# Wider value products, repeated score columns and filler matmuls in a decode attention kernel

## The chip, the cores and the metric

The kernel runs on 1 core of one Trainium2 chip. The metric is the time of one execution on the device in microseconds (us), the median over runs. The profile's span, from the first instruction to the last, is about 2 us shorter than that time.

In the views of the profile PE is TensorE's matmuls, PEld its weight loads, DVE VectorE, ACT ScalarE and POOL GpSimd. "Issue" is time in which the profile shows nothing that the engine waits for. The granted clock is the share of TensorE's full speed that the chip lets it run at; in the clock records of before it is 1.0 or 0.5 and nothing else, in pieces of 3.41 us. "Cold" in the recorded texts is a clock of 0.5. A chunk is 16 of the 64 value products of a unit, one for each quarter of V.

## The reference

Two attention blocks, A and B, decode one token for 4 sequences. Each has 32 query heads and 8 key/value heads of width 128, and a cache of 8192 positions. A uses all positions, B only the last 2048. The outputs are concatenated.

```python
q = (x @ wq)                                   # B, 32 heads, 1, 128
scores = einsum("bhqd,bhkd->bhqk", q, k) * Dh ** -0.5
p = softmax(scores)
o = einsum("bhqk,bhkd->bhqd", p, v)
out = o @ wo                                   # for A and for B, then concatenated
```

There is little arithmetic: the caches that must be read are 168 MB of the 184.6 MB that the kernel reads.

## The kernel before

The work is cut into 40 units: 8 of B and then 32 of A. A unit of A is one sequence and one key/value head: 2 MB of K and 2 MB of V. Four K and four V buffers are filled by one DMA queue, in the order of the units. A unit goes through these steps:

- 32 transposes, which take pairs of bf16 numbers as fp32, bring K into the form that the score product needs; VectorE and ScalarE copy the results to `KT_sb` in turns;
- 64 score products, each with 128 columns of K as weights and 8 query columns streaming;
- softmax over the positions (VectorE, ScalarE, GpSimd);
- 64 value products, each with a 128x128 tile of V as weights and **4** probability columns streaming.

Every product loads new weights (1590 matmuls and 1589 weight loads from 200 to 300 us). TensorE takes the steps of a unit in one fixed order, with the value products of the unit before woven in:

```python
# pe_S: scores
ins = pe.matmul(out=stb[:, t * CPT:(t + 2) * CPT], lhsT=ktv[:, pi, :, e],
                rhs=rhs, start=(e == 0), stop=(e == 1))        # rhs: RQc[:, u % Bn, e, :], 8 columns
# pe_PV: values; CPT is 4 for A
for i in range(TQ):
    t = c * TQ + i
    s, j = t // J, t % J
    ins = pe.matmul(out=otb[:, s * CPT:(s + 1) * CPT], lhsT=V_sb[:, vs, t, :],
                    rhs=pt_cols(u, t * CPT, CPT), start=(j == 0), stop=(j == J - 1))
# (cut) order of TensorE in a unit:
TOKENS = [("T", 0), ("T", 1), ("OT",), ("T", 2), ("T", 3), ("S", 0), ("S", 1), ("X",),
          ("T", 4), ("T", 5), ("S", 2), ("S", 3), ("PV", 0), ("PV", 1), ("OL",),
          ("T", 6), ("T", 7), ("S", 4), ("S", 5), ("PV", 2), ("PV", 3), ("S", 6), ("S", 7), ("OPJ",)]
# (cut) after the last unit L = 39:
for c in range(NQ):
    pe_PV(L - 1, c)
add(dve_norm(L - 1))
for c in range(NQ):          # the V of the last unit comes in four quarters, one DMA each
    pe_PV(L, c)
add(dve_norm(L))
pe_OPJ(L // Bn)              # output projection of the last group: 8 matmuls of 256 columns
```

The body (units 10 to 37) is a hardware loop on TensorE; units 38 and 39 and the end are written out.

## Time and profile before

| | before |
|---|---|
| time, median of 3 runs | 450.13 us |
| span of the profile | 447.8 us |
| mean granted TensorE clock | 0.797 of full |
| DMA share from 50 to 400 us | 1.00 to 1.01 |
| last quarter of V lands (semaphore of its last of 16 parts) | 440.63 us |
| from there to the end | 7.14 us |

From the page of the kernel before: the granted clock and the DMA share in 40 slices (tenths), the summary of the chain that ended last, and two groups (busy us, mean ns of one; then the idle time before them and what ended it). L332 is the transpose, L397 the value product.

```profile
PEclk9996569989886899866596689867875986788596
DMA  8999999999999999999999999999999999999991
...
DMA 54%; PE 35%; issue 4%; ACT 3%; DVE 2%; POOL 0%; ACTq 0%; POOLq 0%
...
L332 PE MATMUL ps<-identf,K_sb 128*128 128x128 f32 x1280 | 217.1, 329 | 32.9 <-DMA K_sb<-in_A_k_cache_dram 17.5
...
L397 PE MATMUL ps<-PT,V_sb 128*128 128x4 bf16 (+1 forms) x2560 | 76.2, 165 | 3.6 <-DMA V_sb<-in_A_v_cache_dram 1.8
```

DMA is full (9 tenths or more) in every slice but the first and the last. The chain is 54% DMA. TensorE is busy too, but it sat idle for 17.5 us before transposes because K was not there: in the body it waits for the stream. The mean of a transpose is 329 ns, which counts time that overlaps with its neighbours (1280 times 329 ns are 421 us, and the group was busy for 217.1 us) and mixes two clocks.

The table of stretches of the kernel before (first column the stretch, then its length, the busy time of each engine with the number of instructions, the granted clock, the DMA share and GB/s):

```profile
core 0: us, PE busy (x) PEld busy (x) DVE busy (x) ACT busy (x) POOL busy (x), PEclk, DMA share, GB/s
200.00:300.00 100.00, 91.00 (x1590) 85.02 (x1589) 44.59 (x103) 43.45 (x50) 9.01 (x29) 0.76 1.01 428
300.00:400.00 100.00, 91.90 (x1660) 84.16 (x1656) 44.40 (x102) 44.23 (x51) 9.69 (x31) 0.77 1.01 428
413.00:427.00 14.00, 13.65 (x174) 11.51 (x175) 5.43 (x14) 3.98 (x6) 0.94 (x3) 0.52 1.00 426
427.00:440.00 13.00, 11.87 (x255) 11.23 (x253) 7.70 (x17) 8.41 (x10) 1.71 (x5) 1.00 0.85 349
440.00:448.00 8.00, 5.17 (x126) 4.10 (x126) 2.08 (x7) 0.42 (x1) 0.46 (x2) 0.50 0.01 3
```

Through the body the stream runs at 428 GB/s. Look at 413 to 427: TensorE is busy 13.65 of 14 us and its clock is 0.52. It has work, and it does it at half speed, just before the end. From 440 on nothing is loaded any more and the kernel still needs almost 8 us.

The timeline of the kernel before, at the end, transposes of the last unit (L332), value products (L397), normalisation (L592), output projection (L474) and final addition (L812):

```profile
start us, us, engine line op out<-in xcount [idle before <-releaser]
...
431.81 2.08 PE L332 MATMUL ps<-identf,K_sb 128*128 128x128 f32 x16
...
438.96 0.39 PE L397 MATMUL ps<-PT,V_sb 128*128 128x4 bf16 x10
...
440.17 3.31 PE L397 MATMUL ps<-PT,V_sb 128*128 128x4 bf16 x118 [0.82 <-issue]
...
443.52 0.17 DVE L592 TENSOR_TENSOR OTg<-ps,RL 128x4 bf16<-128x4 f32 x1 [1.33 <-PE ps L397]
...
443.79 1.86 PE L474 MATMUL ps<-W,OTg 128*4 128x256 bf16 x8 [0.31 <-DVE OTg L592]
...
445.69 0.41 DVE L812 TENSOR_TENSOR xo_sb<-ps,oacc 4x256 bf16<-4x256 f32 x1 [0.44 <-PE ps L474]
```

The last K had landed at 425.79, and its transposes begin only at 431.81. The last V is there at 440.63. TensorE begins its last 118 value products at 440.17 and needs until 443.48 for them, at about 28 ns each. The 0.82 us of "issue" before them come on top. Then the projection takes 1.86 us at half clock.

### The profile page before, as it was taken

The page shows a single profiled execution, that of the slowest core. Times are in us where ns is not written, and L with a number is a line of the kernel's source. Part 1 is how long each engine was busy: PE and PEld are TensorE (multiplying, and loading weights), DVE is VectorE, ACT ScalarE, POOL GpSimd, SP SyncE. Part 2 cuts the span into 40 slices and gives each one's busy share as a digit, 9 for nine tenths or more (in the row PEclk, how much of TensorE's full clock was granted, in tenths as well). Part 3 has the DMA queues.
Part 4 walks back from the last instruction along what each step waited for, and adds up shares of the span by engine and source line. Part 5 has one row for each costly group of instructions (what it writes and reads, how often), then busy time and mean ns, then how long its engine had stood idle before and what let it go on. Part 6 is the DMA issues. An engine that isn't in the chain of part 4 may idle for free.

```text
span 447.8 us, 14767 instructions
## 1 busy us (share of the span) xinstructions
PE 373.4 (83%) x6783; PEld 339.4 (76%) x6783; DVE 195.9 (44%) x451; ACT 179.2 (40%) x202; POOL 40.1 (9%) x126
## 2 busy tenths in 40 slices
PE   0685199899676999988998998899889998988997
PEld 0685199768561898878898887879878987878896
DVE  0354055656440455434363444344443544344363
ACT  1163045435330464434264434334442543435261
POOL 1100000001100011000010001000110100010010
PEclk9996569989886899866596689867875986788596
DMA  8999999999999999999999999999999999999991
GB/s 337 411 415 438 413 421 415 420 421 423 423 422 421 425 422 425 424 429 427 427 427 430 430 424 426 430 428 427 429 426 427 426 430 429 426 424 430 430 403 65
DMA packets 17270, 185.01 MB, mean 413 GB/s; under 512 B 1860, under 2 KB 2392, under 8 KB 4824
## 3 DMA queue, kind: packets, MB, share of 16 engines
q1 hardware_dynamic: 15096, 178.27, 94.4%
q10 hardware_dynamic: 2080, 6.30, 3.5%
q8 instruction: 22, 0.36, 0.3%
q14 instruction: 8, 0.07, 0.0%
q0 software_dynamic: 64, 0.01, 0.0%
HBM read 184.56 MB, written 0.01 MB: 412 GB/s over the span
## 4 chain that ended last, share of the span: by engine, by line
DMA 54%; PE 35%; issue 4%; ACT 3%; DVE 2%; POOL 0%; ACTq 0%; POOLq 0%
DMA K_sb<-in_A_k_cache_dram 41%; PE ps L332 19%; DMA W<-in_A_wq_dram 7%; DMA W<-in_B_wo_dram 6%; PE ps L397 6%; PE ps L371 5%; PE ps L483 3%; ACT KT_sb L341 3%; PE ps L278 1%; DVE KT_sb L340 1%; DVE Dt L543 0%; DVE M L505 0%; ACT PT L554 0%; PE ps L474 0%; PE ps L438 0%
## 5 line engine op out<-in xcount | busy, mean ns | idle before, releaser
L341 ACT ACTIVATE KT_sb<-ps 128x1024 bf16<-128x1024 bf16 x160 | 163.0, 1023 | 244.9 <-PE ps L332 243.1
L332 PE MATMUL ps<-identf,K_sb 128*128 128x128 f32 x1280 | 217.1, 329 | 32.9 <-DMA K_sb<-in_A_k_cache_dram 17.5
L332 PEld LDWEIGHTS ps<-identf,K_sb 128*128 128x128 f32 x1280 | 179.0, 170 | 46.2 <-DMA K_sb<-in_A_k_cache_dram 18.6
L340 DVE COPY KT_sb<-ps 128x512 int32<-128x512 int32 x160 | 110.4, 690 | 138.9 <-PE ps L332 137.7
L397 PE MATMUL ps<-PT,V_sb 128*128 128x4 bf16 (+1 forms) x2560 | 76.2, 165 | 3.6 <-DMA V_sb<-in_A_v_cache_dram 1.8
L371 PEld LDWEIGHTS ps<-RQc,KT_sb 128*128 128x128 bf16 x2048 | 72.9, 100 | 4.5 <-ACT KT_sb L341 1.2
L371 PE MATMUL ps<-RQc,KT_sb 128*128 128x8 bf16 x2048 | 74.3, 167 | 0.9 <-ACT KT_sb L341 0.8
L397 PEld LDWEIGHTS ps<-PT,V_sb 128*128 128x128 bf16 x2560 | 70.8, 97 | 3.9 <-DMA V_sb<-in_A_v_cache_dram 2.0
L575 POOL PARTITION_ALL_REDUCE LB<-L x40 | 17.3, 432 | 155.2 <-DVE L L566 155.2
L514 POOL PARTITION_ALL_REDUCE MB<-M x32 | 11.9, 371 | 173.3 <-DVE M L505 173.3
L483 PE MATMUL ps<-W,OL 128*4 128x512 bf16 x60 | 22.5, 537 | 4.8 <-DMA W<-in_B_wo_dram 4.8
L592 DVE TENSOR_TENSOR OTg<-ps,RL 128x4 bf16<-128x4 f32 (+1 forms) x40 | 6.9, 173 | 40.2 <-PE ps L397 40.2
L505 DVE TENSOR_REDUCE M<-ps 128x4 f32<-128x256 f32 (+1 forms) x40 | 19.1, 477 | 10.8 <-PE ps L371 10.8
L566 DVE TENSOR_REDUCE L<-PT 128x4 f32<-128x256 bf16 (+1 forms) x40 | 21.9, 547 | 3.3 <-ACT PT L554 2.8
L371 PE MATMUL ps<-RQB,KT_sb 128*128 128x16 bf16 x512 | 18.6, 171 | 2.1 <-issue 1.2
L371 PEld LDWEIGHTS ps<-RQB,KT_sb 128*128 128x128 bf16 x512 | 17.9, 99 | 3.0 <-issue 1.5
L554 ACT ACTIVATE PT<-Dt 128x256 bf16<-128x256 f32 (+1 forms) x40 | 18.1, 452 | 4.0 <-DVE Dt L543 2.0
L483 PEld LDWEIGHTS ps<-W,OL 128*4 128x4 bf16 x60 | 5.6, 104 | 15.3 <-issue 8.7
L278 PE MATMUL ps<-xT,W 128*128 128x4 bf16 x256 | 7.4, 165 | 10.9 <-DMA W<-in_A_wq_dram 10.6
L278 PEld LDWEIGHTS ps<-xT,W 128*128 128x128 bf16 x256 | 7.0, 101 | 11.1 <-DMA W<-in_A_wq_dram 10.7
L543 DVE TENSOR_TENSOR Dt<-ps,MB 128x256 f32<-128x256 f32 x32 | 13.3, 415 | 0.5 <-POOL MB L514 0.5
L257 PE MATMUL ps<-ident,xo_sb 4*128 4x4 bf16 x8 | 0.6, 170 | 14.2 <-POOL identf L617 14.2
(49 smaller groups left out, 64.6 us busy)
## 6 DMA issues: line engine op xcount, KB each, us to landing
K_sb<-in_A_k_cache_dram SPq DMA_DIRECT2D x32, 2048.0 KB, 32.0
V_sb<-in_A_v_cache_dram SPq DMA_DIRECT2D x31, 2048.0 KB, 36.0
K_sb<-in_B_k_cache_dram SPq DMA_DIRECT2D x16, 1024.0 KB, 28.2
V_sb<-in_B_v_cache_dram SPq DMA_DIRECT2D x16, 1024.0 KB, 28.2
W<-in_B_wq_dram SPq DMA_DIRECT2D x1, 4096.0 KB, 12.9
W<-in_A_wq_dram SPq DMA_DIRECT2D x1, 4096.0 KB, 30.0
W<-in_A_wo_dram ACTq DMA_DIRECT2D x8, 512.0 KB, 10.5
W<-in_B_wo_dram SPq DMA_DIRECT2D x1, 2048.0 KB, 29.1
```

The source lines that it names most:

```text
L278: ins = pe.matmul(out=bk[:, hl * Bn:(hl + 1) * Bn], lhsT=W1wq[:, c, hq * DH:(hq + 1) * DH], rhs=xT[:, P, c, :], start=(c == 0), stop=(c == ...
L332: ins = pe.transpose(out=bkf[:, pi * 128:(pi + 1) * 128], in_=K_sbf[:, slot, t0:t0 + 2, :].rearrange("p t d -> p (t d)"), identity=identf[ ...
L340: return e.tensor_copy(out=KT_sb.bitcast(I32)[:, tj % NKT, :], in_=bkf.bitcast(I32)[:, :])
L341: return e.activation(out=KT_sb[:, tj % NKT, :], in_=bk[:, :], func=ACTF.Copy)
L371: ins = pe.matmul(out=stb[:, t * CPT:(t + 2) * CPT], lhsT=ktv[:, pi, :, e], rhs=rhs, start=(e == 0), stop=(e == 1))
L397: ins = pe.matmul(out=otb[:, s * CPT:(s + 1) * CPT], lhsT=V_sb[:, vs, t, :], rhs=pt_cols(u, t * CPT, CPT), start=(j == 0), stop=(j == J - 1))
L483: ins = pe.matmul(out=opb[0:Bn, 0:D], lhsT=OL[:, i // REP, i % REP, :], rhs=wo_view[:, wg + i // REP, i % REP, :], start=(P == 1 and first ...
L505: return dve.tensor_reduce(out=M1[:, 0:NC].rearrange("p (s h) -> p s h", h=CPT), in_=stb[:, 0:NT * CPT].rearrange("p (s j h) -> p s h j", ...
L543: return dve.tensor_tensor(out=Dt[:, 0:NT * CPT].rearrange("p (s j h) -> p s j h", s=S, h=CPT), in0=stb[:, 0:NT * CPT].rearrange("p (s j h ...
L554: return act.activation(out=PT[:, u % NPT, 0:NW], in_=Dt[:, 0:NW], func=ACTF.Exp, scale=scale)
L566: return dve.tensor_reduce(out=L1[:, 0:NC].rearrange("p (s h) -> p s h", h=CPT), in_=PT[:, u % NPT, 0:NT * CPT].rearrange("p (s j h) -> p ...
L575: return pool.partition_all_reduce(LB[:, 0:NC], L1[:, 0:NC], channels=128, reduce_op=ReduceOp.add)
```

## The change

The intent: keep TensorE's granted clock up by letting it stream more columns. The value product streams 64 columns instead of 4; only the first 4 of each 64 output columns mean anything. The A score product repeats its 8 query columns 4 times (32 columns); the surplus output is overwritten by the next product. Two matmuls of 512 columns whose result nobody reads ("fillers") stand after each of the first three chunks of the last unit.

```diff
+    NW = 64
+    NR = 4
-        PT = sb("PT", [128, NPT, NT * 2 * REP], BF16)
+        PT = sb("PT", [128, NPT, NT * 2 * REP + NW], BF16)
 ... (cut: filler(), pe_filler(n): n matmuls of 512 columns into a free bank)
-                            rhs = RQc[:, u % Bn, e, :]
+                            rhs = RQc[:, u % Bn, e:e + 1, :].broadcast_to([128, NR, 2 * CPT])
+                            dst = stb[:, t * CPT:(t + 2 * NR) * CPT].rearrange("p (a c) -> p a c", a=NR)
-                    ins = pe.matmul(out=otb[:, s * CPT:(s + 1) * CPT], lhsT=V_sb[:, vs, t, :],
-                                    rhs=pt_cols(u, t * CPT, CPT), start=(j == 0), stop=(j == J - 1))
+                    ins = pe.matmul(out=otb[:, s * NW:(s + 1) * NW], lhsT=V_sb[:, vs, t, :],
+                                    rhs=pt_cols(u, t * CPT, NW), start=(j == 0), stop=(j == J - 1))
 ... (cut: normalisation reads every 64th group; PT is set to 0 at the start)
         for c in range(NQ):
             pe_PV(L, c)
+            if c < NQ - 1:
+                pe_filler(2)
```

## The prediction

> **What bounds the kernel now.** The DMA stream. The table of stretches shows DMA share 1.00 to 1.01 and 414 to 428 GB/s from 50 to 400 us. The chain of waits is 54% DMA. A unit's K and V land every 10.1 us. TensorE waits for K in 13 units (17.5 us, view of waits). So TensorE time matters only at the end. The last quarter of V lands at 440.6 us; the span is 447.8. In those 7.2 us (timeline): TensorE is behind, still issuing the last 118 narrow value products at 440.17 to 443.48 (28 ns each); normalisation 0.17; output projection 1.86 at half clock; addition to 446.10; output DMA about 1.7.

> **What changes.**
> - Value product, 64 per unit: 4 columns to 64. Now 32 take 0.80 us. [...]
> - A score product, 64 per unit: 8 to 32 columns. 16 take 0.38 us now[...].
> - Fillers: 6 matmuls of 512 columns, two after each of the last unit's first three chunks[...]. V quarters land at 436.9, 438.1, 439.4 and 440.6[...].
> - One memset on GpSimd, 128x2304: about 2.3 us (512 columns took 0.52). It may delay the first transposes, but loads are queued about 28 us ahead: worth 0.

> **Critical path.** The stream is untouched: last landing stays at 440.6 +-0.5. [...] TensorE still waits for K and the clock will still drop sometimes, but for fewer pieces: mean clock from 0.80 to about 0.88. That is off the path. In the tail, TensorE should have done all but the last chunk when it lands: chunk to 441.15, normalisation to 441.4, projection at full clock about 1.0 to 442.45, addition to 442.9, output to 444.6. Gain about 3.2 us: 2.3 from the backlog, 0.85 from the projection.

> **Prediction: 447.0 us, 8 in 10 within 445.8 to 449.0.** Faster by over 2%: 0.01; within 2%: 0.96; slower by over 2%: 0.03.

> **What the profile would show.** Right: last V landing near 440.6; granted clock 1.00 from about 427 to the end; the chain ending with the V DMA, then 16 value products, projection about 1.0 us. Wrong: a clock of 0.5 at the projection; more than one chunk of value products after the last landing; fillers delaying chunks; slices with DMA below 9.

> **What would make it wrong.** If in cold stretches wide products[...] cost more than the activity buys back, TensorE falls behind before 427 us and the tail keeps its length: about 450. [...] the gain shrinks to the 1 to 2 us that the fillers give. [...]

The forecast's sum came to a gain of 3.2 us, from a span of 447.8 to one of 444.6: 2.3 of backlog and 0.85 of projection. None of them is a term of the 3.2 us by itself, but the 0.55 us that the forecast gives the last chunk seems to lean on the first. It stands, as does the 1.0 us for a projection that took 1.86 us at half clock, as the author's estimate (measured: 0.64 and 1.03).

What the two traces show, as medians from one start to the next within a piece of the clock: a product of 4 or 8 columns 25 ns at full clock and 27 at half, one of 32 columns 25 and 27, one of 64 columns 29 and 53, one of 512 columns 215 to 217 and 427. A transpose takes 109 and 213 ns, as does a product of 256 columns in the projection; so the count of a transpose as 256 columns fits its time. Whether the chip counts it so is not shown.

## The result, and the profile after

The ratio is the mean time of one kernel's runs over that of the other's of the same rounds, so not quite the ratio of the medians that stand beside it. Executions over 1.5% slower than the fastest of the same kernel are left out of the means.

| | before | after |
|---|---|---|
| time, median of 4 runs each (before: the three above and one more) | 450.04 us (448.51 to 450.60) | 447.92 us (447.24 to 448.72) |
| ratio | | 0.9961, 95% interval 0.9939 to 0.9982 |
| span of the profiled run | 447.8 us | 445.2 us |
| mean granted clock | 0.797 | 0.942 |
| last V lands | 440.63 us | 441.03 us |
| from there to the end | 7.14 us | 4.16 us |
| value products begun after that landing | 101 | 16 |
| output projection | 1.86 us | 1.03 us |

The same parts of the page after (L348 is now the transpose, L414 the value product):

```profile
PEclk9998579999976899989899899999899999999999
DMA  8999999999999999999999999999999999999993
...
DMA 57%; PE 32%; issue 4%; ACT 3%; DVE 3%; POOL 1%; ACTq 0%; POOLq 0%
...
L348 PE MATMUL ps<-identf,K_sb 128*128 128x128 f32 x1280 | 183.8, 292 | 36.0 <-DMA K_sb<-in_A_k_cache_dram 19.5
...
L414 PE MATMUL ps<-PT,V_sb 128*128 128x64 bf16 x2560 | 90.4, 195 | 17.5 <-DMA V_sb<-in_A_v_cache_dram 16.1
```

DMA is as full as before. The clock is mostly full. A transpose takes 292 ns on average instead of 329, which is 33 us less in the sum of transposes; a value product, 195 instead of 165. Almost none of these 33 us shows in the time, because the stream sets the pace in the body: instead, TensorE now also waits 16.1 us for V.

The same stretches after:

```profile
core 0: us, PE busy (x) PEld busy (x) DVE busy (x) ACT busy (x) POOL busy (x), PEclk, DMA share, GB/s
200.00:300.00 100.00, 82.47 (x1622) 75.81 (x1620) 45.04 (x105) 43.69 (x50) 9.50 (x31) 0.97 1.01 428
300.00:400.00 100.00, 80.80 (x1618) 74.92 (x1618) 43.30 (x99) 43.58 (x50) 9.01 (x29) 0.98 1.01 427
413.00:427.00 14.00, 12.76 (x226) 11.30 (x226) 7.48 (x20) 7.21 (x9) 1.51 (x5) 1.00 1.02 431
427.00:440.00 13.00, 12.29 (x295) 11.41 (x294) 6.74 (x16) 5.79 (x7) 1.60 (x4) 1.00 0.85 351
440.00:446.00 6.00, 2.75 (x44) 1.71 (x41) 0.99 (x3) 0.00 (x0) 0.00 (x0) 1.00 0.02 5
```

The clock from 413 to the end is 1.00, and the instruction counts show what it did for TensorE: 226 matmuls instead of 174 between 413 and 427.

The timeline at the end of the kernel after, transposes of the last unit (L348), fillers (L321), value products (L414), normalisation (L610), projection (L491), final addition (L834):

```profile
428.57 2.08 PE L348 MATMUL ps<-identf,K_sb 128*128 128x128 f32 x16
...
438.78 0.59 PE L321 MATMUL ps<-RQA,ident 128*128 128x512 bf16 x2
...
439.21 0.63 PE L414 MATMUL ps<-PT,V_sb 128*128 128x64 bf16 x16
...
439.68 0.60 PE L321 MATMUL ps<-RQA,ident 128*128 128x512 bf16 x2
...
440.11 0.63 PE L414 MATMUL ps<-PT,V_sb 128*128 128x64 bf16 x16
...
440.58 0.60 PE L321 MATMUL ps<-RQA,ident 128*128 128x512 bf16 x2
441.07 0.52 PEld L414 LDWEIGHTS ps<-PT,V_sb 128*128 128x128 bf16 x16 [0.39 <-DMA V_sb<-in_A_v_cache_dram]
441.07 0.64 PE L414 MATMUL ps<-PT,V_sb 128*128 128x64 bf16 x16
441.75 0.17 DVE L610 TENSOR_TENSOR OTg<-ps,RL 128x4 bf16<-128x4 f32 x1 [2.54 <-PE ps L414]
...
442.02 1.03 PE L491 MATMUL ps<-W,OTg 128*4 128x256 bf16 x8 [0.31 <-DVE OTg L610]
...
443.09 0.41 DVE L834 TENSOR_TENSOR xo_sb<-ps,oacc 4x256 bf16<-4x256 f32 x1
```

The last K landed at 425.98 and its transposes begin at 428.57, 2.6 us later instead of 6.0. Now the last 16 value products wait for the landing of V: their weight loads (PEld) stood idle for 0.39 us until it came. Their 0.64 us, the normalisation, a projection at full clock and the addition are all that is left.

### The profile page after: what moved, and what is told of

Read it like the earlier page. It is cut to its first block, busy times and chain, and to the rows that moved or that the text cites. A ratio compares the mean times of both kernels' runs of the same rounds, so it can differ in the third digit from the quotient of the medians.

```text
span 445.2 us, 14780 instructions
## 1 busy us (share of the span) xinstructions
PE 350.6 (79%) x6789; PEld 318.4 (72%) x6789; DVE 195.3 (44%) x451; ACT 178.9 (40%) x202; POOL 42.0 (9%) x127
## 4 chain that ended last, share of the span: by engine, by line
DMA 57%; PE 32%; issue 4%; ACT 3%; DVE 3%; POOL 1%; ACTq 0%; POOLq 0%
DMA K_sb<-in_A_k_cache_dram 44%; PE ps L348 15%; PE ps L414 7%; DMA W<-in_A_wq_dram 7%; DMA W<-in_B_wo_dram 6%; PE ps L389 5%; ACT KT_sb L357 3%; PE ps L500 2%; PE ps L280 1%; DVE KT_sb L356 1%; DVE M L522 1%; DVE Dt L560 1%; ACT PT L571 1%; POOL PT L628 0%; PE ps L455 0%
## 5 line engine op out<-in xcount | busy, mean ns | idle before, releaser
L348 PE MATMUL ps<-identf,K_sb 128*128 128x128 f32 x1280 | 183.8, 292 | 36.0 <-DMA K_sb<-in_A_k_cache_dram 19.5
L348 PEld LDWEIGHTS ps<-identf,K_sb 128*128 128x128 f32 x1280 | 147.4, 148 | 49.7 <-DMA K_sb<-in_A_k_cache_dram 21.1
L414 PE MATMUL ps<-PT,V_sb 128*128 128x64 bf16 x2560 | 90.4, 195 | 17.5 <-DMA V_sb<-in_A_v_cache_dram 16.1
L414 PEld LDWEIGHTS ps<-PT,V_sb 128*128 128x128 bf16 x2560 | 81.9, 99 | 19.9 <-DMA V_sb<-in_A_v_cache_dram 17.7
L389 PE MATMUL ps<-RQc,KT_sb 128*128 128x32 bf16 x2048 | 76.1, 177 | 1.0 <-ACT KT_sb L357 1.0
L389 PEld LDWEIGHTS ps<-RQc,KT_sb 128*128 128x128 bf16 x2048 | 72.0, 97 | 4.0 <-ACT KT_sb L357 1.3
L610 DVE TENSOR_TENSOR OTg<-ps,RL 128x4 bf16<-128x4 f32 (+1 forms) x40 | 6.9, 174 | 44.8 <-PE ps L414 44.8
L500 PE MATMUL ps<-W,OL 128*4 128x512 bf16 x60 | 17.2, 435 | 3.6 <-DMA W<-in_B_wo_dram 3.6
L389 PEld LDWEIGHTS ps<-RQB,KT_sb 128*128 128x128 bf16 x512 | 17.7, 98 | 2.2 <-ACT KT_sb L357 0.9
L280 PEld LDWEIGHTS ps<-xT,W 128*128 128x128 bf16 x256 | 7.0, 101 | 11.9 <-DMA W<-in_A_wq_dram 11.5
L259 PE MATMUL ps<-ident,xo_sb 4*128 4x4 bf16 x8 | 0.5, 169 | 16.1 <-POOL identf L637 16.1
```

The lines of the kernel that those rows point to most:

```text
L280: ins = pe.matmul(out=bk[:, hl * Bn:(hl + 1) * Bn], lhsT=W1wq[:, c, hq * DH:(hq + 1) * DH], rhs=xT[:, P, c, :], start=(c == 0), stop=(c == ...
L348: ins = pe.transpose(out=bkf[:, pi * 128:(pi + 1) * 128], in_=K_sbf[:, slot, t0:t0 + 2, :].rearrange("p t d -> p (t d)"), identity=identf[ ...
L389: ins = pe.matmul(out=dst, lhsT=ktv[:, pi, :, e], rhs=rhs, start=(e == 0), stop=(e == 1))
L414: ins = pe.matmul(out=otb[:, s * NW:(s + 1) * NW], lhsT=V_sb[:, vs, t, :], rhs=pt_cols(u, t * CPT, NW), start=(j == 0), stop=(j == J - 1))
L500: ins = pe.matmul(out=opb[0:Bn, 0:D], lhsT=OL[:, i // REP, i % REP, :], rhs=wo_view[:, wg + i // REP, i % REP, :], start=(P == 1 and first ...
```

## The experiments

Twelve runs followed, in three jobs of four; two of them repeat the kernels before and after. Kernels of one job share a chip and the runs of the kernel before; the three jobs ran on three chips, so ratios, not times, are compared across jobs. One quantity besides the times explains nearly all of them: how long after the landing of the last K its transposes begin ("lag" below; worked out from the landing records and the instruction starts of each trace). The lag says how far TensorE is behind the stream when the stream ends.

| kernel | ratio to before, 95% interval | mean clock | lag at the last K, us | value products begun after the last landing | projection, us | last landing, us | span, us |
|---|---|---|---|---|---|---|---|
| before | | 0.797 | 6.0 | 101 | 1.86 | 440.63 | 447.8 |
| before_again | one look | 0.783 | 7.0 | 118 | 1.86 | 441.10 | 449.0 |
| after | 0.9961 | 0.942 | 2.6 | 16 | 1.03 | 441.03 | 445.2 |
| after_again | 0.9960 (0.9938 to 0.9982) | 0.950 | 2.6 | 16 | 1.03 | 441.05 | 445.2 |
| no_fill | 0.9952 (0.9932 to 0.9972) | 0.946 | 4.0 | 38 | 1.03 | 440.90 | 445.7 |
| body_only | 0.9952 (0.9938 to 0.9966) | 0.950 | 2.6 | 16 | 1.86 | 440.82 | 445.8 |
| pv_only | 0.9940 (0.9924 to 0.9957) | 0.939 | 2.6 | 16 | 1.03 | 440.99 | 445.1 |
| s_only | 0.9965 (0.9949 to 0.9982) | 0.849 | 3.6 | 16 | 1.86 | 440.94 | 445.9 |
| reorder_wide | 0.9942 (0.9927 to 0.9956) | 0.954 | 3.8 | 26 | 1.03 | 440.87 | 445.3 |
| fill_only | 1.0074 (1.0051 to 1.0097) | 0.791 | 4.6 | 48 | 1.86 | 441.06 | 449.1 |
| tail_only | 1.0035 (1.0013 to 1.0057) | 0.813 | 5.2 | 64 | 1.03 | 441.02 | 447.8 |
| reorder_narrow | 1.0003 (0.9987 to 1.0018) | 0.773 | 7.1 | 118 | 1.86 | 441.35 | 449.2 |
| nw128 | 1.0265 (1.0237 to 1.0293) | 0.978 | 11.3 | 192 | 1.03 | 440.82 | 458.5 |
| dense_extra | 1.0271 (1.0220 to 1.0321) | 0.927 | 15.8 | 192 | 1.86 | 440.97 | 457.3 |

The landing stays within 440.6 and 441.4 us in all fourteen traces, whatever the kernel does on TensorE. So the stream is untouched, and all the differences lie in what is left to do after it.

The lag of the earlier units, worked out in the same way, says which clock counts. In every trace but those of nw128 and dense_extra the lag is 0.0 at the K of units 36 and 37: TensorE has caught up and waits. So what is left at the end comes from the clock after the K of unit 37 has landed at about 411 us, not from the mean clock. Count the pieces of 3.41 us at half clock between 410 us and the first transposes of the last unit:

| half-clock pieces after 410 us | kernels | lag at the last K, us |
|---|---|---|
| 0 | after, after_again, body_only, pv_only | 2.6 |
| 1 | no_fill, s_only, reorder_wide | 3.6 to 4.0 |
| 2 | fill_only | 4.6 |
| 3 | tail_only | 5.2 |
| 4 | before | 6.0 |
| 5 | before_again, reorder_narrow | 7.0 and 7.1 |

Each piece at half clock costs 0.6 to 1.4 us of lag.

### First job: which part gained, and is it repeated

**after_again**: the changed kernel unaltered.

> The changed kernel again, to see how far its own runs spread and what spreads them. Theory A (the last landing of V is now the start of everything that remains): the span is the last landing plus about 4.15 us in every trace, so a trace with a span near 447 has its last landing near 442.8; ratio to before 0.994 to 0.997. Rival (something in TensorE's tail varies, for instance the clock at the output projection): the last landing stays at 441.0 and the distance from it to the end varies.

Measured: 447.19 us (447.00 to 448.57, 6 runs), ratio 0.9960. The trace has the landing at 441.05 and the end 4.18 us later. This agrees with theory A as far as the trace goes; the profiled run was a quick one. Of the ten timed runs of this kernel, seven have spans of 445.2 to 445.7 and three of 446.8 to 447.0; none of the three was traced, so what lengthens them is open.

**no_fill**: the change without the fillers.

```diff
-            if c < NQ - 1:
-                pe_filler(2)
```

> Wide value products and repeated score columns, no fillers. Theory A: TensorE has done all but the last chunk when it lands, so the backlog part of the gain (2.3 us predicted) stays; the last 6 us before the landing then hold about 2800 counted columns per 3.41 us piece, at the edge, so the clock at the projection may be 0.5 (projection 1.9 instead of 1.03 us, last chunk 0.85 instead of 0.64): span 0 to 1.2 us over the changed kernel's. Rival R1 (the fillers are what gained): the time goes back to that of before, ratio 1.00.

Measured: 447.21 us (446.86 to 447.42), ratio 0.9952. The fillers are not what gained (R1 falls): without them the clock at the projection is still 1.00 (1.03 us). (The 0.85 us that the expectation gives a last chunk at half clock is 16 of the 53 ns that a product of 64 columns takes there in the trace of after.) In this trace the clock was 0.5 for one 3.41 us piece at 413.7, so its lag at the last K is 1.4 us longer than in the trace of after and 38 value products were left; without fillers among them, that cost only 0.6 us.

**fill_only**: the kernel before, with the fillers alone.

> The kernel before with the six fillers only. Theory A: the clock stays at 0.5 around 413 to 427 us, TensorE is still behind at the last landing, and the fillers then stand in its way: three pairs of 0.43 us (0.86 if cold) against 0.85 us saved at the projection: same as before within 1 us, if anything slower; ratio 0.999 to 1.002. Rival R1 (the fillers are what gained): ratio 0.996.

Measured: 452.22 us (451.14 to 453.81), ratio 1.0074. The expectation had the direction but not the size. Timeline of fill_only at the end, fillers (L319), value products (L411), projection (L488):

```profile
441.25 0.63 PE L319 MATMUL ps<-RQA,ident 128*128 128x512 bf16 x1 [0.24 <-issue]
...
441.67 0.61 PE L411 MATMUL ps<-PT,V_sb 128*128 128x4 bf16 x16
...
442.14 1.01 PE L319 MATMUL ps<-RQA,ident 128*128 128x512 bf16 x2
...
442.95 0.61 PE L411 MATMUL ps<-PT,V_sb 128*128 128x4 bf16 x16
...
443.43 1.01 PE L319 MATMUL ps<-RQA,ident 128*128 128x512 bf16 x2
...
444.23 0.61 PE L411 MATMUL ps<-PT,V_sb 128*128 128x4 bf16 x16
...
445.15 1.86 PE L488 MATMUL ps<-W,OTg 128*4 128x256 bf16 x8 [0.31 <-DVE OTg L606]
```

TensorE is behind at the landing (441.06), the fillers stand between it and its work, and the clock is low, so a pair holds the next chunk up by about 0.8 us (442.14 to 442.95) instead of 0.43 (439.68 to 440.11 in after; the 0.86 of the expectation is about two of the 427 ns that 512 columns take at half clock in the traces of before and after). Their six times 512 columns do not bring the clock back either: the projection still takes 1.86 us. In the trace of after, the pair before the last chunk fell into time in which TensorE would have waited; here none does. One of the six fillers has no record in this trace.

**tail_only**: wide value products for the last three units, repeated score columns for the last two, fillers kept, everything in the loop as before.

```diff
+                            nr = NR if u >= L - 1 else 1
+                nw = NW if u >= L - 2 else CPT      # and slices [s * NW : s * NW + nw]
```

> Wide value products only for the last three units, repeated score columns only for the last two, fillers kept; the loop is as before. Theory A: the cold stretch at 413 to 427 us lies in the loop and stays, so TensorE is still behind at the last landing, and only the projection gets faster: gain 0 to 1 us, ratio 0.998 to 1.000. Rival R3 (only what happens after 427 us counts, the backlog is made good in the tail): the gain of the whole change, 0.996.

Measured: 450.80 us (449.56 to 451.40), ratio 1.0035, slightly slower than expected. The clock is 0.5 for most of 411.7 to 425.4, the lag 5.2 us, and all 64 value products of the last unit, and with them all six fillers (five have a record), follow the landing. The projection is fast (1.03) and cannot pay for that. So R3, the whole gain from the tail, falls. That the wide products in the tail do not help at all is not shown: this kernel carries the fillers, which alone cost 0.74%, and it is faster than fill_only (1.0035 against 1.0074). A wide tail without fillers was not run.

### Second job: the body, and another way to be on time

**before_again**: the kernel before, traced again.

> The kernel before, traced once more, for its tail. Theory B (the tail of before depends on where the 3.41 us clock pieces fall; the trace that the prediction was read from had 0.5 over all of 413 to 427 us and is among its slowest runs): in a trace with another position of the pieces, another number of value products is left after the last landing, and the span differs by up to 2.5 us at the same last landing (441.0 +-0.3). Rival (the last landing moves the span): the distance from the last landing to the end stays 7.1 us.

Measured: one run of 450.71 us (its state is unknown). In this trace the clock is 0.5 from 410.9 to 428.0, 118 value products come after the landing, and the distance from the landing to the end is 7.88 us instead of 7.14. So the distance does vary, by 0.74 us here; the pause before the last 118 value products now ends after the landing, at 441.40. But the trace that the prediction was read from was not among the slowest: the spans of the 29 timed runs of before in the three jobs go from 446.0 to 448.8, and 447.8 lies in the middle. That half of theory B is wrong.

**body_only**: wide for all but the last units, no fillers.

```diff
+                            nr = NR if u < L - 1 else 1
+                nw = NW if u < L - 2 else CPT
-            if c < NQ - 1:
-                pe_filler(2)
```

> Wide value products for all units but the last three, repeated score columns for all but the last two, no fillers. Theory A: the clock is 1.0 over most of 413 to 427 us, so TensorE is nearly on time; in the tail only the clock at the projection is open (1.03 or 1.86 us). Ratio 0.995 to 0.998, span 445 to 447. If the width mattered in the tail, as the fillers were meant to, 0.999 or more.

Measured: 447.56 us (447.39 to 447.77), ratio 0.9952. Timeline of body_only at the end, value products (L416) and projection (L493):

```profile
439.63 0.59 PE L416 MATMUL ps<-PT,V_sb 128*128 128x4 bf16 x16 [0.64 <-DMA V_sb<-in_A_v_cache_dram]
...
440.87 0.58 PE L416 MATMUL ps<-PT,V_sb 128*128 128x4 bf16 x16 [0.65 <-DMA V_sb<-in_A_v_cache_dram]
...
441.76 1.86 PE L493 MATMUL ps<-W,OTg 128*4 128x256 bf16 x8 [0.31 <-DVE OTg L612]
```

With narrow products in the tail TensorE is on time all the same: it waits for the last two quarters of V. The clock has fallen, and that costs 0.83 us at the projection and nothing else. So the width in the body does the main thing, and the width in the tail buys 0.83 us at the projection in the trace. In the times this does not stand out: no_fill, which is wide in the tail too, has the same ratio (0.9952).

**reorder_narrow**: the kernel before with the value products of unit 37 moved behind the scores of unit 39.

```diff
-            return None if u == L - 1 else L - 2
+            return None
 ...
+        for v in (L - 2, L - 1):
+            for c in range(NQ):
+                pe_PV(v, c)
+            add(dve_norm(v))
```

> The kernel before, all matmuls narrow, with one change of order: the value products of the third-last unit come after the scores of the last unit, so TensorE need not wait for that V in the midst of the last unit. Theory A (what counts is only that TensorE has done all but the last chunk when the last V lands; the clock is one means to that): the scores of the last unit end near 434 us even at a low clock, 16 to 26 value products are left after the landing at 441.0, the projection takes 1.86 or 1.03 us: span 445.2 to 446.5, ratio 0.994 to 0.998. Rival (the gain needs the high clock itself): ratio 1.000.

Measured: 449.69 us (449.56 to 450.91), ratio 1.0003. My expectation failed, and the number is the rival's. The trace shows why: the clock was 0.5 from 412.1 to 429.1, the lag at the last K is 7.1 us, and the transposes of the last unit end at 438.16 instead of 434. The wait for that V had cost nothing before, because TensorE reached it after it had landed. The kernel therefore did not make TensorE punctual, and did not test whether punctuality at a low clock would gain.

**reorder_wide**: the same order with wide products, no fillers.

> The same order with wide value products and repeated score columns, no fillers. Theory A: TensorE waits for each quarter of V in every run, span is the last landing plus 4.15 us, about 445.2, and its runs spread less than those of the changed kernel; ratio 0.994 to 0.996. If the waits for the quarters let the clock fall, the projection takes 1.86 us and the span is 446.

Measured: 447.10 us (446.75 to 447.49), ratio 0.9942. The trace has 26 value products after the landing and ends 4.40 us after it, close to the 4.15 expected; the projection takes 1.03 us. The six runs spread by 0.7 us, against 1.6 us for after_again. But no_fill has the same small spread (0.6 us) in the old order, so it is the missing fillers that go with it, not the order.

### Third job: the dose

**pv_only**: wide value products, scores as before, no fillers (`NR = 1`).

> Wide value products (64 columns) in all units, score products as before, no fillers. By the column count (transpose 256, value product 64, score product 8) a unit streams 12800 columns against 14336 in the whole change and 8960 in the kernel before. Theory A: most of the clock comes back, mean 0.90 to 0.95, TensorE on time at the end: ratio 0.995 to 0.998.

Measured: 447.18 us (446.86 to 447.64), ratio 0.9940, clock 0.939. The wide value product alone gives the whole gain, so neither the repeated score columns nor the fillers are needed for it; the ratio is a little better than I expected.

**s_only**: only the repeated score columns (`NR = 4` in the kernel before).

> Score products of A repeated to 32 columns, value products narrow, no fillers. 10496 columns a unit against 8960 before. Theory A: the clock rises a little, mean 0.80 to 0.87, TensorE is still behind at the end in most runs: ratio 0.997 to 1.000. Rival (the repeat matters as much as the wide value product): 0.996 or less and a clock of 0.93 or more.

Measured: 448.19 us (447.60 to 448.75), ratio 0.9965, clock 0.849. The clock is where it was expected, the ratio slightly better: a lag of 3.6 us is already short enough to leave only 16 value products after the landing. What stays is the slow projection (1.86 us). The interval of the ratio overlaps that of the change (0.9939 to 0.9982), though the mean clock is far lower (0.849 against 0.942): only one half-clock piece fell between 410 us and its last unit.

**dense_extra**: all products narrow; eight dummy matmuls of 512 columns before the value products of each unit.

```diff
+                if c == 0 and u < L - 2:
+                    for _ in range(8):
+                        pe.matmul(out=otb[:, 0:512], lhsT=ident[:, :], rhs=..., start=True, stop=True)
```

> The kernel before, all products narrow, with eight dummy matmuls of 512 columns put before the value products of each unit but the last three (result overwritten). 13056 columns a unit. Theory A (the clock follows streamed columns, whatever matmul streams them, and the clock is all that the width buys): mean clock 0.92 or more, TensorE on time, ratio 0.995 to 0.998, although TensorE does 1.7 us more work a unit. Rival (the wide value product itself helps, or added work on TensorE hurts): 1.000 or more.

Measured: 462.11 us (458.98 to 473.50; the run of 473.50 is slow and left out of the ratio), ratio 1.0271. Half of the expectation held: the clock rose to 0.927 with every value product narrow, so streamed columns raise it, also when dummy matmuls stream them. The other half failed: the time rose. (The 1.7 us of the expectation is eight of the 216 ns that 512 columns take at full clock in the trace of before.)

**nw128**: the change with `NW = 128`.

> The whole change with 128 columns a value product. [...] Theory A: clock 0.97 or more, still on time[...]: ratio 0.995 to 0.998. If TensorE time counted through the body, [...] ratio 1.05 or more.

Measured: 461.21 us (460.74 to 463.25), ratio 1.0265, where I had expected a gain. In the trace the products start 55.7 ns apart and the last chunk takes 1.06 us. The stretches of nw128 in the body and at the end:

```profile
200.00:300.00 100.00, 96.36 (x1666) 91.69 (x1663) 44.56 (x103) 43.88 (x51) 9.58 (x31) 1.00 1.01 428
300.00:400.00 100.00, 94.32 (x1609) 88.63 (x1608) 44.27 (x103) 43.66 (x50) 9.20 (x30) 1.00 1.01 428
...
440.00:458.00 18.00, 16.06 (x270) 14.70 (x268) 4.48 (x13) 3.32 (x4) 1.23 (x3) 1.00 0.01 3
```

The clock is full, DMA share and GB/s are those of the changed kernel, and the last V lands at 440.82; yet the kernel needs another 17.7 us after it. The lags say how. TensorE enters the long A part far behind, because it is held up by the output projection of B, whose weights land only at 137 us (145 in nw128): at unit 10 the lag is 11.5 us in before, 11.0 in after and 20.0 in nw128. From there the changed kernel catches up in three units (11.0, 8.0, 4.8, 1.1). A lag of that size can be made good: the trace of reorder_narrow has 19.2 at unit 10 and 0.0 at unit 17. nw128 is at 14.2 by unit 14, but from there it gains only about 0.7 us in four units (9.9 at unit 38), and at the last K it is still 11.3 us behind. Four units land in 40.4 us, and its TensorE needs 39.7 us for four: three take 9.1 us each, and the fourth takes 12.4, with the head-group work and the turn of the loop, which I had forgotten. In dense_extra the same happens (19.9 at unit 10, 15.8 at the end). So both halves count: the columns must be streamed, and they must cost almost no time.

A version that beats both kernels clearly was not found. pv_only and reorder_wide have the lowest ratios (0.9940 and 0.9942), but their intervals overlap that of the change, and they ran on other chips.

## Why the prediction was right, point by point

The predicted time was 447.0 us, 445.8 to 449.0; measured were 447.92 in the first runs and 447.19 in after_again. The forecast of a change within 2% held, but it would have held for no change at all, and the range up to 449.0 takes in some runs of the kernel before (447.75 to 450.56 in the first job). It is the traces, not the time, that test the mechanism.

- *The stream is the bound, and its end does not move.* Right: 440.6 to 441.4 us in every trace.
- *The clock falls because narrow products stream too little.* Shown: pv_only, s_only and dense_extra raise it in three different ways (from 0.797 to 0.939, 0.849 and 0.927), fillers in the tail alone leave it at 0.79. How the backlog follows from it is shown by the table of half-clock pieces above. The author's counts of columns per piece of 3.41 us, made from the clock records and the starts of the matmuls, predicted the sense of the steps. In the trace of before, of the pieces at full clock the 21 that were followed by 0.5 held 336 to 3272 columns (median 2384), the 50 that were followed by 1.0 held 2908 to 7680; of those at half clock the 20 followed by 1.0 held 3248 to 4096, the 32 others 0 to 3072. The fall did not need idle time: four of the 21 came after pieces in which the profile shows TensorE busy throughout (at 204.5, 245.5, 296.7 and 395.6 us, 2560 to 2832 columns). In one place transposes alone brought the clock back: the piece at 146.5 us holds 16 of them and no other matmul, and the next has a clock of 1.0. In the trace of before all but 2 of 123 pieces of 3.41 us obey the two thresholds of the prediction (up from about 3200 columns, down under about 2850), in that of after all but 2 of 123, in that of s_only all but 9 of 123, in that of tail_only, the worst, all but 10 of 123. The thresholds were read from the trace of before, so only the other traces test them; they are limits of a count, with these exceptions, and not a mechanism shown. The mean clock was underestimated, 0.942 against 0.88.
- *What a wide value product takes.* Measured: 32 take 0.94 to 1.01 us in the chain of after; at full clock they start 29.0 to 29.5 ns apart, at half clock 53.
- *TensorE finishes all but the last chunk.* Right in both traces of the changed kernel: 16 left. In no_fill and reorder_wide, 38 and 26, because one low piece still fell just there.
- *The memset is worth 0.* Right: it takes 2.02 us, the first matmul starts 1.9 us later (16.06 instead of 14.19) and the lag at unit 10 is no larger.
- *The size of the gain.* Too large. Predicted 3.2 us: 2.3 of backlog and 0.85 of projection. Between the two traces the time from the landing to the end of the value products fell from 2.85 to 0.68 us, 2.17, and the projection by 0.83. Part of the 2.17 us is not the products' own time: the pause of 0.82 us stood just before the last 118 of them in before, and in after it came 4 us before the landing. The missing 0.4 us is the landing: it was 440.63 in the trace that I read and is 441.0 in nearly all others, the second trace of before (441.10) included, so the change did not move it. That leaves 2.6 us between the traces. The timed runs gave 2.1 us in the medians (1.7 in after_again's job). The three longer runs in ten of the changed kernel make up part of that. They are about 1.5 us longer, and no run of the three kernels with wide value products in all units and without fillers (16 runs, 446.75 to 447.64) is like them; a TensorE that comes late and then has three pairs of 0.43 us in its way would look so. That is argued from fill_only and tail_only, where it is seen, and not shown in a trace of the changed kernel.
- *"the gain shrinks to the 1 to 2 us that the fillers give."* That was wrong: the fillers alone cost 0.74%, and taking them out of the change costs nothing (0.9952 against 0.9960).

What stays open: whether the three longer runs are due to fillers, what a wide tail without fillers gains by itself, and whether a punctual TensorE at a low clock would gain the rest (reorder_narrow failed to make it punctual).

## What to carry to other kernels

In a kernel bound by a stream, as this one is, an engine off the bound still mattered twice: it must have caught up when the stream ends (7.14 against 4.16 us were left after the last landing), and it needs slack to catch up after every hold-up (nw128 had 39.7 us of work for 40.4 us of stream and stayed behind). Read its lag behind the landings unit by unit, not its busy share. Here 60 more columns in a value product cost 4 ns at full clock (4 columns took 25 ns, 64 took 29) and brought the mean clock from 0.797 to 0.939 (pv_only); going further (128, 56 ns) turned a gain of 0.4% into a loss of 2.7%, and no run showed a gain from fillers.
